# Block-sparse attention feeding a Fourier-mix MLP: the gate product of half the head pairs in 16-bit matmuls instead of float32

## The chip, the cores and the metric

The kernel runs on one NeuronCore of a Trainium2 chip. The metric is the device time of one execution, in microseconds; lower is better. The engines run side by side, each through its own queue in order: TensorE (PE in the profile, its weight loads PEld) multiplies into PSUM; VectorE (DVE), ScalarE (ACT) and GpSimd (POOL) work element by element; SyncE (SP) issues most DMAs.

## What is computed

For 4 batches and 8 heads, with 768 positions and 64 dimensions, attention in which a query sees the causal part of its own block of 64 positions and of up to three other blocks that a gate picks:

```python
k_rep = k.reshape(B, H, n_blocks, block, D).mean(axis=3)          # 12 block means
gate_scores = np.einsum('bhsd,bhnd->bhsn', q, k_rep)              # the gate product
gate_scores = np.where(causal, gate_scores, -1000000000.0)
top_idx = np.argsort(gate_scores, axis=-1)[..., -top_k:]          # top_k = 3
...                                                               # mask from top_idx and own block
attn = softmax(0.125 * q @ k.T, masked);  x = attn @ v            # heads side by side: (4, 768, 512)
X = np.fft.fft(np.fft.fft(x, axis=1), axis=2)
u = x + np.real(X)
un = (u - mean(u)) / sqrt(var(u) + 1e-6)
out = u + np.maximum(un @ w_ch1, 0.0) @ w_ch2                     # 512 -> 2048 -> 512
```

Inputs and output are float32. The choice of blocks is discrete: a gate score that changes its rank changes the output, so the kernel keeps the gate product in float32 while all other products are in 16 bits.

## The kernel before

Two heads of one batch make a pair; 16 pairs (kk = 0 to 15, four to a batch) are worked one after the other, 128 partitions holding 2 x 64 head dimensions. The stages of a pair are spread over three turns of the loop over pairs, so that each engine has work of several pairs at hand:

- stage_A (two turns ahead): TensorE transposes k and q of the pair, three blocks of 128x128 at a time, into PSUM tiles tp. VectorE copies q out as float32, qT (L264), and sums k over blocks of 64, kr12 (L270); two small copies lay these sums out as kr24, one head beside the other with zeros between (L275). ScalarE casts k to 16 bits into kI (L282, for the first seven pairs VectorE takes one of the four, L280). GpSimd casts qT into qg (L267), the 16-bit operand of the scores, one for each head.
- stage_B (two turns ahead, after stage_A): the gate product g, five matmuls of 128 rows of qT (weights) with kr24 (24 columns moving), all float32 (L291; block row 0 needs none). VectorE adds the causal constant (L294), finds the largest eight of each 12 (L301), and makes a 0/1 mask gmp of blocks that are dropped (L303, L306).
- stage_C (one turn ahead): TensorE transposes gmp into gt; VectorE copies it into 12 extra rows of qg (L315). The scores' matmul then adds -60000 to dropped blocks through 12 extra rows of kI that hold -60000 in the columns of one block each.
- stage_S: the scores of a head in three sections of 896 columns, ScalarE's exponential with scale 0.125 into ptl (L349). The causal diagonal is masked by a matmul for pairs up to 6 and on VectorE after (L355).
- stage_AV: ptl times v into av (L370), divided by the row sum on VectorE (L374, L375), into x.

When a batch's four pairs are done, its second half is queued: sums and differences on GpSimd and VectorE (fs, ft, fo, fc; L383 to L389), the Fourier products (za, ya; mx; stage_S1 and stage_S2), u and its statistics on VectorE (L459, L461, L462), the reciprocal root of the variance on GpSimd (stage_N, down to rstd and nmr, L483 to L490), the normalised x on VectorE and ScalarE (L493, L497), its transposes (unt, L506), and the two products of the MLP (ha and hb, L522; ch, L536), with their evictions (L525 on ScalarE, L527 and L539 on VectorE).

The order on TensorE and GpSimd is written out by the program: the loop over pairs emits the stages, and between them a planner, `filler`, hands out units of the second half of earlier batches. It keeps a clock of estimated costs (`feed.now`), by which units that depend on others become ready; `main(stage, cost, ...)` emits a stage and moves that clock by its cost. VectorE, ScalarE and SyncE are ordered by a scheduler.

PSUM has eight banks: four rotate among all tiles with tag ps (tp, g, gt, av, unt, ha, hb, ch, mx, ...), two double ones hold the scores. A tile's buffer comes free when its last reader is done; which earlier tile's buffer a new one gets is fixed when the program is built.

Of the kernel before, what the change touches and what calls it, by code (L numbers as in the profile page):

```python
# [12 lines left out]
F16 = mybir.dt.float16  # L13
# [3 lines left out]
AF = mybir.ActivationFunctionType  # L17
# [101 lines left out]
def kernel(  # L119
# [24 lines left out]
    MULT = mybir.AluOpType.mult  # L144
    ADD = mybir.AluOpType.add
# [6 lines left out]
    psump = ctx.enter_context(tc.tile_pool(name="psum", bufs=4, space=bass.MemoryType.PSUM))  # L152
    apool = ctx.enter_context(tc.tile_pool(name="attn", bufs=2))
    bpool = ctx.enter_context(tc.tile_pool(name="bat", bufs=1))
    spool = ctx.enter_context(tc.tile_pool(name="small", bufs=8))

    def pst(shape, name, dtype=FP, tag="ps", bufs=None):
        return psump.tile(shape, dtype, tag=tag, name=name, bufs=bufs)

    def const(shape, dtype, name):  # L160
        return cpool.tile(shape, dtype, tag=name, name=name)
# [25 lines left out]
    qg_t = [[const([128, S], F16, f"qg_{e}_{sl}") for sl in range(3)] for e in range(2)]  # L187
    warm = const([128, 512], F16, "warm")
    kr24_t = [const([128, 2 * NB], FP, f"kr24_{sl}") for sl in range(2)]
    gmp_t = [const([128, NST - 1, 2, 32], F16, f"gmp_{sl}") for sl in range(2)]  # L190


    EARLY = 7

    feed = Feed()
    P = [dict() for _ in range(NK)]
# [29 lines left out]
    def pool_after(t):  # L226
        nc.gpsimd.tensor_copy(out=dummyp[0:1, 0:1], in_=t[0:1, 0:1])
# [19 lines left out]
    def stage_A(kk, who, g):  # L247
        d = P[kk]
        src = d["qn"] if who == 0 else d["kn"]
        if who == 0 and g == 0:  # L250
            d["qt"] = apool.tile([128, S], FP, tag="qT32", name=f"qT32_{kk}")
            d["qg"] = [qg_t[e][kk % 3] for e in range(2)]
        if who == 1 and g == 0:
            d["kI"] = [kI_t[e][kk % 3] for e in range(2)]
            d["kr12"] = spool.tile([128, NB], FP, tag="kr12", name=f"kr12_{kk}", bufs=2)
            d["kr24"] = kr24_t[kk % 2]
        ps = pst([128, 3, 128], f"tp_{kk}_{who}_{g}")
        for i in range(3):
            nc.tensor.transpose(ps[:, i, :],  # L259
                                src[:, 3 * g + i, :, :].rearrange("p h d -> p (h d)"), id32)  # L260
        flat = ps.rearrange("p a c -> p (a c)")
        cols = slice(384 * g, 384 * (g + 1))
        if who == 0:
            nc.vector.tensor_copy(out=d["qt"][:, cols], in_=flat)  # L264
            if g == 1:
                for e in range(2):
                    nc.gpsimd.tensor_copy(out=d["qg"][e][0:64, :],  # L267
                                          in_=d["qt"][64 * e:64 * e + 64, :])
        else:
            nc.vector.tensor_reduce(out=d["kr12"][:, 6 * g:6 * g + 6],  # L270
                                    in_=ps.rearrange("p a (x c) -> p a x c", x=2),
                                    axis=mybir.AxisListType.X, op=ADD)
            if g == 1:
                for e in range(2):
                    nc.vector.tensor_copy(out=d["kr24"][64 * e:64 * e + 64, NB * e:NB * (e + 1)],  # L275
                                          in_=d["kr12"][64 * e:64 * e + 64, :])
            for e in range(2):
                dst, src_ = d["kI"][e][0:64, cols], flat[64 * e:64 * e + 64]
                if kk < EARLY and g == 1 and e == 1:
                    nc.vector.tensor_copy(out=dst, in_=src_)  # L280
                else:
                    nc.scalar.copy(out=dst, in_=src_)  # L282
# [3 lines left out]

    def stage_B(kk):
        d = P[kk]
        gps = pst([128, NG, 2 * NB], f"g_{kk}")
        for st in range(1, NST):  # L290
            nc.tensor.matmul(gps[:, st - 1, :], d["qt"][:, 128 * st:128 * (st + 1)], d["kr24"],  # L291
                             start=True, stop=True)
        gsb = apool.tile([128, NG, 2, NB], FP, tag="gsb", name=f"gsb_{kk}")
        nc.vector.tensor_tensor(out=gsb.rearrange("p s e n -> p s (e n)"), in0=gps,  # L294
                                in1=cz24[:, 1:NST, :], op=ADD)
        gmp = gmp_t[kk % 2]
        d["gmp"] = gmp
        mx8 = spool.tile([128, NG, 2, 8], FP, tag="mx8", name=f"mx8_{kk}", bufs=2)
        for st in range(NG):
            for e in range(2):  # L300
                nc.vector.max(out=mx8[:, st, e, :], in_=gsb[:, st, e, :])  # L301
        gm = gmp[:, :, :, 0:NB]
        nc.vector.tensor_tensor(out=gm, in0=gsb,  # L303
                                in1=mx8[:, :, :, 2:3].to_broadcast([128, NG, 2, NB]),
                                op=mybir.AluOpType.is_lt)
        nc.vector.tensor_tensor(out=gm, in0=gm, in1=oth24[:, 1:NST, :, :], op=MULT)  # L306

    def stage_C(kk):
        d = P[kk]
# [24 lines left out]
    def stage_S(kk, e, s):  # L334
        d = P[kk]
        if s == 0:
            d.setdefault("pt", {})[e] = apool.tile([128, 3 * SEC], F16, tag=f"ptl{e}",
                                                   name=f"ptl_{kk}_{e}")
        pt = d["pt"][e]
        sp = pst([128, 1024], f"sc_{kk}_{e}_{s}", tag="sc", bufs=2)  # L340
        by_pe = kk < EARLY
        for (jt, a0, a1, co) in SECS[s]:
            diag = by_pe and a0 == 128 * jt
            nc.tensor.matmul(sp[:, co:co + (a1 - a0)],  # L344
                             d["kI"][e][0:76, 128 * jt:128 * (jt + 1)],
                             d["qg"][e][0:76, a0:a1], start=True, stop=not diag)
            if diag:
                nc.tensor.matmul(sp[:, co:co + 128], id16, ltri, start=False, stop=True)  # L348
        nc.scalar.activation(out=pt[:, SEC * s:SEC * (s + 1)], in_=sp[:, 0:SEC], func=AF.Exp,  # L349
                             scale=0.125)  # L350
        if s == 2 and not by_pe:
            um = ut01.rearrange("p (o c) -> p o c", o=1).to_broadcast([128, 3, 128])
            for dg in (pt.rearrange("p (t c) -> p t c", t=3)[:, :, 0:128],
                       pt[:, 384:].rearrange("p (t c) -> p t c", t=3)[:, :, 384:512]):
                nc.vector.tensor_tensor(out=dg, in0=dg, in1=um, op=MULT)  # L355
# [235 lines left out]
    def main(fn, cost, *a):  # L591
        fn(*a)
        feed.spend(cost)
# [6 lines left out]
    with tc.manual_schedule(engines={mybir.EngineType.PE, mybir.EngineType.Pool}):  # L600
# [52 lines left out]
        for kk in range(NK):  # L653
            for p in range(6):
# [70 lines left out]
```

## Time and profile before

| | us |
|---|---|
| runs shown | 345.65, 347.63, 347.56; median 347.56 |
| the profiled execution | 346.12 |
| its span in the profile | 344.3 |
| granted TensorE clock, mean over the span | 0.979 of full |
| product g, 160 records in all | TensorE 20.6 busy, weight loads 20.5 |
| qT copies, 32 in all (VectorE) | 16.6, 547 ns each |
| qg casts, 32 in all (GpSimd) | 27.2, 849 ns each |
| kI casts, 57 on ScalarE | 27.0, 473 ns each |

How to read it: the span is that of one execution taken by the hardware profiler. Each line of a group gives the source line, the engine and operation, what is written and read, the number of instructions, their summed busy time and the mean of one. A float32 matmul appears as two records with a weight load each, so the five matmuls of a pair's g are ten. The chain of waits is followed back from the last instruction: at each step to what released it, or to the instruction before it on the same engine. "Idle before, releaser" names what an engine waited for. The products g of pairs 8 to 15 start on the chain at 89.27, 109.82, 131.23, 152.22, 170.69, 191.40, 212.87 and 233.25 us.

### The profile page before, as it was taken

The page shows a single profiled execution, that of the slowest core. Times are in us where ns is not written, and L with a number is a line of the kernel's source. Part 1 is how long each engine was busy: PE and PEld are TensorE (multiplying, and loading weights), DVE is VectorE, ACT ScalarE, POOL GpSimd, SP SyncE. Part 2 cuts the span into 40 slices and gives each one's busy share as a digit, 9 for nine tenths or more (in the row PEclk, how much of TensorE's full clock was granted, in tenths as well). Part 3 has the DMA queues.
Part 4 walks back from the last instruction along what each step waited for, and adds up shares of the span by engine and source line. Part 5 has one row for each costly group of instructions (what it writes and reads, how often), then busy time and mean ns, then how long its engine had stood idle before and what let it go on. Part 6 is the DMA issues. An engine that isn't in the chain of part 4 may idle for free.

```text
span 344.3 us, 6929 instructions
## 1 busy us (share of the span) xinstructions
PE 320.4 (93%) x2688; PEld 210.2 (61%) x2688; DVE 229.1 (67%) x701; ACT 172.7 (50%) x259; POOL 93.5 (27%) x177
## 2 busy tenths in 40 slices
PE   7899994998899989999999989899999999899995
PEld 3577772886766666566566766556666655456442
DVE  2788889788565779887566688986544868533211
ACT  3177885497874853454375653442566210344000
POOL 8435664244543020342215030161012100200000
PEclk9999998799699999999999999999999999999999
DMA  9999999966498440433523000011000011100021
GB/s 173 197 211 208 261 183 219 147 143 138 80 172 144 82 93 17 107 107 89 143 48 74 20 2 30 32 44 51 32 0 2 5 58 61 62 2 0 32 89 64
DMA packets 85312, 31.18 MB, mean 91 GB/s; under 512 B 77736, under 2 KB 81136, under 8 KB 85280
## 3 DMA queue, kind: packets, MB, share of 16 engines
q1 hardware_dynamic: 79984, 25.88, 33.2%
q0 software_dynamic: 3552, 4.40, 8.1%
q10 hardware_dynamic: 1744, 0.46, 0.7%
q8 instruction: 21, 0.34, 0.4%
q14 instruction: 11, 0.09, 0.1%
HBM read 28.63 MB, written 6.29 MB: 101 GB/s over the span
## 4 chain that ended last, share of the span: by engine, by line
PE 74%; DVE 12%; ACT 4%; POOL 4%; issue 3%; DMA 2%; ACTq 0%; POOLq 0%; DVEq 0%
PE ch L536 21%; PE ha L522 15%; PE hb L522 8%; PE sc L344 8%; PE g L291 5%; PE av L370 5%; PE tp L259 3%; ACT kI L282 2%; DVE kr L270 2%; DVE mx L301 2%; DMA qn<-in_q_dram 2%; PE gt L312 1%; PE ya L424 1%; PE mx L448 1%; DVE bst L461 1%
## 5 line engine op out<-in xcount | busy, mean ns | idle before, releaser
L349 ACT ACTIVATE ptl<-sc 128x896 f16<-128x896 f32 x96 | 87.1, 917 | 51.9 <-PE sc L344 42.1
L536 PE MATMUL ch<-w_sb,hT 128*128 128x512 f16 x384 | 91.2, 379 | 1.3 <-DVE u L539 1.2
L522 PEld LDWEIGHTS <-w_sb 128*128 128x128 f16 x512 | 48.8, 98 | 35.7 <-issue 0.7
L522 PE MATMUL ha<-unT,w_sb 128*128 128x512 f16 x256 | 65.7, 379 | 0.1
L344 PE MATMUL sc<-qg,kI 76*128 76x512 f16 (+3 forms) x256 | 55.7, 309 | 4.1 <-ACT ptl L349 4.0
L536 PEld LDWEIGHTS <-hT 128*128 128x128 f16 x384 | 36.1, 97 | 36.8 <-issue 1.4
L525 ACT ACTIVATE hT<-ha 128x512 f16<-128x512 f32 x64 | 38.1, 597 | 30.7 <-PE ha L522 30.7
L527 DVE TENSOR_SCALAR hT<-hb 128x256 f16<-128x256 f32 x64 | 26.9, 422 | 36.1 <-PE hb L522 36.1
L522 PE MATMUL hb<-unT,w_sb 128*128 128x256 f16 x256 | 38.4, 273 | 0.3 <-ACT unT L509 0.3
L383 POOL TENSOR_TENSOR fs<-x 128x384 f16<-128x384 f16 x12 | 11.2, 929 | 100.2 <-DVE x L375 100.2
L344 PEld LDWEIGHTS <-kI 76*128 76x128 f16 x256 | 24.5, 101 | 19.4 <-issue 2.9
L282 ACT CAST kI<-tp 64x384 f16<-64x384 f32 x57 | 27.0, 473 | 11.7 <-DVE kr L270 10.7
L267 POOL CAST qg<-qT 64x768 f16<-64x768 f32 x32 | 27.2, 849 | 19.7 <-DVE qT L264 18.7
L539 DVE TENSOR_TENSOR u<-ch,u 128x512 f32<-128x512 f32 x24 | 16.5, 688 | 21.6 <-PE ch L536 21.3
L370 PE MATMUL av<-v,ptl 128*128 128x65 f16 x672 | 26.2, 195 | 0.0
L370 PEld LDWEIGHTS <-ptl 128*128 128x128 f16 x672 | 24.8, 98 | 2.1 <-issue 0.2
L497 ACT ACTIVATE x<-u,nmr,rstd 128x512 f16<-128x512 f32 x12 | 8.9, 803 | 26.8 <-POOL nmr L490 26.8
L270 DVE TENSOR_REDUCE kr<-tp 128x6 f32<-128x384 f32 x32 | 17.0, 546 | 7.0 <-PE tp L259 6.9
L291 PEld LDWEIGHTS g<-kr,qT 128*128 128x128 f32 x160 | 20.5, 200 | 1.3 <-issue 0.3
L291 PE MATMUL g<-kr,qT 128*128 128x24 f32 x160 | 20.6, 271 | 0.0
L348 PE MATMUL sc<-ltri,id 128*128 128x128 f16 x84 | 18.6, 222 | 0.0
L375 DVE TENSOR_TENSOR x<-av,rcp 128x384 f16<-128x384 f32 x32 | 17.8, 557 | 1.0
(91 smaller groups left out, 406.5 us busy)
## 6 DMA issues: line engine op xcount, KB each, us to landing
vn<-in_v_dram SPq DMA_DIRECT2D x32, 192.0 KB, 3.6
out_dram<-u SPq DMA_DIRECT2D x24, 256.0 KB, 2.0
kn<-in_k_dram SPq DMA_DIRECT2D x30, 192.0 KB, 4.0
qn<-in_q_dram SPq DMA_DIRECT2D x30, 192.0 KB, 4.1
w_sb<-in_moe_w_ch_dram POOLq DMA_DIRECT2D x8, 256.0 KB, 6.9
w_sb<-in_moe_w_ch_dram POOLq DMA_DIRECT2D x4, 512.0 KB, 8.5
cs_sb<-c_CS SPq DMA_DIRECT2D x1, 289.5 KB, 4.8
ss_sb<-c_SS SPq DMA_DIRECT2D x1, 289.5 KB, 3.6
```

Source lines behind the costliest of these rows:

```text
L267: nc.gpsimd.tensor_copy(out=d["qg"][e][0:64, :], in_=d["qt"][64 * e:64 * e + 64, :])
L270: nc.vector.tensor_reduce(out=d["kr12"][:, 6 * g:6 * g + 6], in_=ps.rearrange("p a (x c) -> p a x c", x=2), axis=mybir.AxisListType.X, op=ADD)
L282: nc.scalar.copy(out=dst, in_=src_)
L291: nc.tensor.matmul(gps[:, st - 1, :], d["qt"][:, 128 * st:128 * (st + 1)], d["kr24"], start=True, stop=True)
L344: nc.tensor.matmul(sp[:, co:co + (a1 - a0)], d["kI"][e][0:76, 128 * jt:128 * (jt + 1)], d["qg"][e][0:76, a0:a1], start=True, stop=not diag)
L348: nc.tensor.matmul(sp[:, co:co + 128], id16, ltri, start=False, stop=True)
L349: nc.scalar.activation(out=pt[:, SEC * s:SEC * (s + 1)], in_=sp[:, 0:SEC], func=AF.Exp, scale=0.125)
L370: nc.tensor.matmul(av[:, st, 0:65], pt[:, o:o + 128], d["v16"][:, e, jt, 0:65], start=(cnt == 0), stop=(cnt == 20))
L522: nc.tensor.matmul(hp_, w1_sb[:, dt, 128 * it:128 * (it + 1)], unT[:, dt, c0:c1], start=(dt == 0), stop=(dt == NDT - 1))
L525: nc.scalar.activation(out=hT[:, c0:c1], in_=hp_, func=AF.Relu)
L527: nc.vector.tensor_scalar(out=hT[:, c0:c1], in0=hp_, scalar1=0.0, scalar2=None, op0=mybir.AluOpType.max)
L536: nc.tensor.matmul(cps, x["hT"][it][:, 128 * st:128 * (st + 1)], w2_sb[:, it, :], start=(it == 0), stop=(it == NIT - 1))
```

## The change

For pairs 8 to 15 (SPLIT = 8) the gate product is done in 16-bit matmuls. q is multiplied by 64 and split into a high part, rounded to f16, and a low part, the f16 of the rest; the block sums of k likewise. The high and low parts of q share the bytes of the float32 tile qT. The parts of k stand side by side, 24 columns each, in a new tile krx, and each block row takes two matmuls, one for either part of q, over all 48 columns, summed in PSUM; VectorE adds the two halves of 24 columns. All four cross terms are so kept. ScalarE makes the high part of q from PSUM, VectorE the low part. qg is cast from the high part, and so is 64 times larger: the mask gets the factor 64 too, and the exponential's scale is divided by it. The planner's cost of stage_B is 0.35 instead of 1.05 for these pairs; a pool of small tiles has 6 buffers instead of 8; GpSimd's wait before the first w2 loads is on the low part.

```diff
-    spool = ctx.enter_context(tc.tile_pool(name="small", bufs=8))
+    spool = ctx.enter_context(tc.tile_pool(name="small", bufs=6))
...
+    krx_t = [const([128, 2, 2 * NB], F16, f"krx_{sl}") for sl in range(2)]
...
+    SPLIT = 8
+    QS = 64.0
+    STT = nc.vector.scalar_tensor_tensor
...
+            if kk >= SPLIT:
+                parts = d["qt"].bitcast(F16)
+                d["qh"], d["ql"] = parts[:, 0:S], parts[:, S:2 * S]
...
-            nc.vector.tensor_copy(out=d["qt"][:, cols], in_=flat)
+            if kk < SPLIT:
+                nc.vector.tensor_copy(out=d["qt"][:, cols], in_=flat)
+            else:
+                nc.scalar.activation(out=d["qh"][:, cols], in_=flat, func=AF.Copy, scale=QS)
+                STT(out=d["ql"][:, cols], in0=flat, scalar=QS, in1=d["qh"][:, cols], op0=MULT, op1=SUB)
             if g == 1:
                 for e in range(2):
                     nc.gpsimd.tensor_copy(out=d["qg"][e][0:64, :],
-                                          in_=d["qt"][64 * e:64 * e + 64, :])
+                                          in_=d["qt" if kk < SPLIT else "qh"][64 * e:64 * e + 64, :])
...
-            if g == 1:
+            if g == 1 and kk < SPLIT:
                 for e in range(2):
                     nc.vector.tensor_copy(out=d["kr24"][64 * e:64 * e + 64, NB * e:NB * (e + 1)],
                                           in_=d["kr12"][64 * e:64 * e + 64, :])
+            elif g == 1:
+                d["krx"] = krx_t[kk % 2]
+                for e in range(2):
+                    r, c = slice(64 * e, 64 * e + 64), slice(NB * e, NB * (e + 1))
+                    hi, lo = d["krx"][r, 0, c], d["krx"][r, 1, c]
+                    nc.vector.tensor_scalar(out=hi, in0=d["kr12"][r, :], scalar1=QS, scalar2=None, op0=MULT)
+                    STT(out=lo, in0=d["kr12"][r, :], scalar=QS, in1=hi, op0=MULT, op1=SUB)
...
+            gps = pst([128, NG, 2, 2 * NB], f"g_{kk}")
+            krx = d["krx"].rearrange("p o n -> p (o n)")
+            for st in range(1, NST):
+                for n, part in enumerate((d["qh"], d["ql"])):
+                    nc.tensor.matmul(gps[:, st - 1, :, :].rearrange("p o n -> p (o n)"),
+                                     part[:, 128 * st:128 * (st + 1)], krx, start=(n == 0), stop=(n == 1))
+            nc.vector.tensor_tensor(out=gsf, in0=gps[:, :, 0, :], in1=cz24[:, 1:NST, :], op=ADD)
+            nc.vector.tensor_tensor(out=gsf, in0=gps[:, :, 1, :], in1=gsf, op=ADD)
...
-        nc.vector.tensor_tensor(out=gm, in0=gm, in1=oth24[:, 1:NST, :, :], op=MULT)
+        if kk < SPLIT:
+            nc.vector.tensor_tensor(out=gm, in0=gm, in1=oth24[:, 1:NST, :, :], op=MULT)
+        else:
+            STT(out=gm, in0=gm, scalar=QS, in1=oth24[:, 1:NST, :, :], op0=MULT, op1=MULT)
...
-                             scale=0.125)
+                             scale=0.125 if kk < SPLIT else 0.125 / QS)
...
+        for t in krx_t:
+            nc.gpsimd.memset(t, 0.0)
...
-                    main(stage_B, 1.05, kk + 2)
+                    main(stage_B, 1.05 if kk + 2 < SPLIT else 0.35, kk + 2)
...
-                pool_after(P[kk + 2]["qt"])
+                pool_after(P[kk + 2]["qt" if kk + 2 < SPLIT else "ql"])
```

In the built program TensorE's stream is the same as before but for g: where a pair from 8 on had five float32 matmuls it has ten 16-bit ones. ScalarE has two more instructions for each of these pairs and VectorE three, GpSimd two more in all.

More of the change, by code (lines that the diff above doesn't have):

```diff
@@ L288, in stage_B @@
         d = P[kk]
[L289 to L292, printed above, removed]
         gsb = apool.tile([128, NG, 2, NB], FP, tag="gsb", name=f"gsb_{kk}")
-        nc.vector.tensor_tensor(out=gsb.rearrange("p s e n -> p s (e n)"), in0=gps,
-                                in1=cz24[:, 1:NST, :], op=ADD)
+        gsf = gsb.rearrange("p s e n -> p s (e n)")
+        if kk < SPLIT:
+            gps = pst([128, NG, 2 * NB], f"g_{kk}")
+            for st in range(1, NST):
+                nc.tensor.matmul(gps[:, st - 1, :], d["qt"][:, 128 * st:128 * (st + 1)], d["kr24"],
+                                 start=True, stop=True)
+            nc.vector.tensor_tensor(out=gsf, in0=gps, in1=cz24[:, 1:NST, :], op=ADD)
+        else:
+            gps = pst([128, NG, 2, 2 * NB], f"g_{kk}")
+            krx = d["krx"].rearrange("p o n -> p (o n)")
+            for st in range(1, NST):
+                for n, part in enumerate((d["qh"], d["ql"])):
[3 more added lines that the diff above has]
+            nc.vector.tensor_tensor(out=gsf, in0=gps[:, :, 1, :], in1=gsf, op=ADD)
         gmp = gmp_t[kk % 2]
@@ L305, in stage_B @@
                                 op=mybir.AluOpType.is_lt)
-        nc.vector.tensor_tensor(out=gm, in0=gm, in1=oth24[:, 1:NST, :, :], op=MULT)
+        if kk < SPLIT:
+            nc.vector.tensor_tensor(out=gm, in0=gm, in1=oth24[:, 1:NST, :, :], op=MULT)
+        else:
+            STT(out=gm, in0=gm, scalar=QS, in1=oth24[:, 1:NST, :, :], op0=MULT, op1=MULT)
     def stage_C(kk):
```

## The prediction

> **What bounds the kernel.** I read the page's busy shares first, then its chain of work that ended last, then that chain in order of time around each gate product (line L291, tile g), and last the waits and the timeline where the chain leaves TensorE.
>
> ```profile
> PE 320.4 (93%) x2688; PEld 210.2 (61%) x2688; DVE 229.1 (67%) x701; ACT 172.7 (50%) x259; POOL 93.5 (27%) x177
> ...
> PEclk9999998799699999999999999999999999999999
> ...
> PE 74%; DVE 12%; ACT 4%; POOL 4%; issue 3%; DMA 2%; ACTq 0%; POOLq 0%; DVEq 0%
> ...
> L370 PEld LDWEIGHTS <-ptl 128*128 128x128 f16 x672 | 24.8, 98 | 2.1 <-issue 0.2
> ...
> L291 PEld LDWEIGHTS g<-kr,qT 128*128 128x128 f32 x160 | 20.5, 200 | 1.3 <-issue 0.3
> ```
>
> TensorE is busy 93% of the span and carries 74% of the chain; the clock row dips twice. A float32 weight load takes 200 ns, a 16-bit one of the same size 98 ns. The 160 records of g are ten for each of 16 pairs. The chain in order of time shows the two settings in which a g can lie:
>
> ```profile
> 87.72 0.58 PE sc L344
> ...
> 89.27 2.07 PE g L291 x10
> ...
> 170.25 0.44 PE hb L522 x4
> 170.69 1.03 PE g L291 x10
> 171.72 0.87 PE ha L522 x4
> ...
> 178.34 0.64 PE av L370 x21
> ...
> 212.87 1.03 PE g L291 x10
> ...
> 214.37 0.69 DVE u L459
> 215.07 0.73 DVE mx L301 x10
> ...
> 218.95 0.61 DVE u L539
> 219.56 0.04 issue
> 219.61 1.02 PE ch L536 x4
> ```
>
> At 170.69 (pair 12) g has matmuls directly before and after it: there, shorter is earlier. At 212.87 (pair 14) the chain leaves TensorE 1.5 us later and VectorE sets the pace until 219.61. At 89.27 (pair 8) the half clock doubles g.
>
> **The change part by part.** *Gate product.* Removed per pair: 1.03 us. Added: ten 16-bit matmuls with 128-column weights, 48 columns moving. The nearest row is av, the same pairing with 65 columns: 21 in 0.64 us, 30 ns each, so 0.30 us for ten. The far bound is gt (five transposes in 0.39 us on the chain, 78 ns each): 0.78 us. I take av's, nearest in shape: a gain of 0.73 us where TensorE is continuous (0.25 by the far bound).
>
> The Trainium skill ("TensorE: Matmul & The Clock Gate", section "Back-to-back issue gap") speaks against this: it gives some 81 ns for each sustained load and matmul pair at 128 columns. By that the ten would cost 0.81 us and the pair gain 0.22; av's 30 ns here contradicts it for narrow operands, so the row decides.
>
> *q.* Two VectorE copies (547 ns each) become two ScalarE activations 128x384 and two VectorE operations reading PSUM and the new 16-bit part. VectorE: 128x384 with two sources is x<-av,rcp, 557 ns: no difference. ScalarE: between kI's cast (64x384, 473 ns) and hT (128x512, 597 ns), say 0.5 us each, 1.0 per pair; ScalarE is idle half the span, so what counts is where they stand in its queue (below). GpSimd's qg now waits for ScalarE's half; its 16-bit read may cost less or more than the 849 ns of now, and in the timeline qg of pair 9 is cast by 103.7 while its scores start two pairs later. GpSimd's casts of v and, at pairs 8 and 9, the w2 loads (issued at 89.4 and 104.7) stand behind it and slip by the same 1 us; w2's product starts at 132.5.
>
> *k and the mask.* Per pair VectorE gets two more 64x12 operations (186 ns as kr's copies), a second add of 128x120 (283 ns as the first) and a fused multiply (217 to 283 ns, was 217): 0.7 us, all in order before whatever stands behind.
>
> *The rest.* The exponential's scale is a constant, no cost. Two small GpSimd memsets before the kI loads cost about 0.15 us each by the v memsets (128 to 152 ns); those loads are issued by 5.5 us and first used at 17.8. Six instead of eight small buffers touch rcp and bst, which the same engine consumes within a microsecond. The estimate of g in the planner's clock changes no place in TensorE's stream: in the built program it is as before but for g itself.
>
> Now pair by pair, as the built order has the new operations.
>
> - Pairs 9, 11, 12, 13 (g at 109.82, 152.22, 170.69, 191.40): TensorE continuous. Transposes end 1.5 to 3 us before the next user of their buffer, in which ScalarE's and VectorE's halves (1.6 us) fit: at pair 13 transposes end at 182.4 and the user starts at 184.23, while VectorE today frees that buffer at 184.05. If the cover is gone it costs some 0.3 us a pair. 4 x 0.73 = 2.9 gained.
> - Pair 8: ScalarE's two stand behind the three x of L497 (which wait for GpSimd's nmr and end at 86.87) and ahead of the exponential that releases the scores at 87.72. So scores start 1.0 later, g at 90.2, and at half clock it lasts 0.6 instead of 2.07: it ends at 90.8 instead of 91.33. Gain 0.4 (bounds: 1.5, loss 1.0).
> - Pair 14: VectorE is saturated from 209.3 to 223.7, so the shorter g ends in a wait. Its own addition ahead of u L539 is 0.3; and the built program puts the ch that waits there at 219.61 in a buffer freed by ScalarE's kI casts, which start at 219.2 today and would start 0.4 later; two take 0.95. ch at 220.6: loss 1.0 (bounds 0 and 1.3).
> - Pair 10 likewise: mx, released today by u L459 at 137.97, waits for two kI casts that start at 137.6: 138.6, loss 0.6 (bounds 0, 0.9).
> - Pair 15: the second q operation moves behind VectorE's x (ends 228.95), and VectorE arrives about 1.2 late at the unT copies after it; of 0.73 I keep 0.5 (bounds 0.73, 0).
>
> Sum: -0.4 - 2.9 + 0.6 + 1.0 - 0.5 = -2.2 us. Nothing after 240 contains the change; the last 100 us only start earlier.
>
> The profiled execution took 346.1 us (span 344.3 plus 1.8); the three runs have a median of 347.6, 345.65 to 347.63. I set the sum against the middle of the two, 346.8: **344.6 us**. By the bounds this case runs from -3.8 (nothing lost at 10 and 14) to +0.6 (gt's price for the matmuls): 343.0 to 347.4.
>
> **Rivals.**
>
> *All eight pay.* If the losses at 10, 14 and 15 don't arise, because VectorE catches up in earlier time that TensorE frees, and 8 gains as the others: 8 x 0.73 = 5.8, so 341.0. For it: 93% busy. Against: 1.25 us of idle already before ch at 219.61 behind VectorE.
>
> *One more half-clock interval.* The rows of the granted clock show 0.50 from 57.0 to 63.8 and from 87.7 to 94.6, both after stretches where TensorE was less than 60% busy (1.9 us of the last 3.4, and 1.5). Pair 14's idle of 1.25 us grows to about 2.1. One such interval of 6.8 us at half clock loses 3.4: -2.2 + 3.4 = +1.2, 348.0. Against it: 12.5 to 16 us is no busier (2.3 of 4 us between 12 and 16) and keeps its clock.
>
> The same page of the Trainium skill ("The two states you'll see") asks for a whole idle window of about 3.4 us before the clock halves; by it 2.1 us of idle costs nothing and the sum stays as it is. The rows here show it halved with some work in the window, so I keep the rival.
>
> *Slower.* The mechanism is the same queueing, decided at two places: ScalarE's casts hold buffers at 138 and at 220 so long that TensorE falls below that share in both, and two intervals follow: -2.2 + 6.8 = +4.6, 351.4. It decides once the waits there exceed some 2 us each; today they are 0.38 and 1.25, which speaks against it.
>
> That the change doesn't do what it says can be ruled out: the built program has ten 16-bit matmuls for each of these pairs and no float32 product.
>
> **How the numbers follow.** Forecast 0.52, all eight pay 0.21, one interval 0.15, slower 0.12. One per cent, about what a measurement of this kernel tells from none, is 3.5 us. Faster by more: all of the second and 0.14 of the forecast, whose lower bound is -3.8: 0.35. Slower: 0.12. Within: 0.53. The range leaves out the slower case and some 0.07 at the lower end of the second: 340.8 to 348.2. The likeliest case alone has 343.0 to 347.4.
>
> **What would show it.** g of pairs 8 to 15 at about 0.30 us on the chain, 0.6 at half clock; 30 ns a matmul. TensorE's busy time down some 5.5 us, VectorE's up by 5 to 6, ScalarE's by about 8. The time between g of pair 9 and g of pair 10 shorter by 0.7; between g of 14 and g of 15 not shorter. Wrong if g's ten take over 0.6 at full clock, if ch near 218 waits no longer than today, or if the clock row has a third dip.

## The result, and the profile after

The changed kernel takes 345.19 us (median of 22 runs, 343.56 to 348.69), the kernel before in the same comparison 346.62 us (22 runs, 345.65 to 350.14). The ratio is 0.9952, with a 95% interval from 0.9935 to 0.997: some 1.5 us less, which is real and lies within the 1% that was called no change. Forecast were 344.6 us, with 340.8 to 348.2. The profiled execution took 346.51 us with a span of 344.7; nine of the 22 had a mean granted clock of 0.98 (median 344.2 us), the other thirteen 0.968 to 0.975 (345.59), and the profiled one is of the thirteen.

The page's busy shares, clock row and chain by engine:

```profile
PE 316.1 (92%) x2688; PEld 204.9 (59%) x2688; DVE 234.0 (68%) x725; ACT 178.9 (52%) x275; POOL 94.0 (27%) x179
...
PEclk9989998799899989999999999999999999999999
...
PE 69%; DVE 24%; ACT 3%; issue 2%; POOL 2%; DVEq 0%; ACTq 0%
```

TensorE's busy time went down by 4.3 us, VectorE's up by 4.9, ScalarE's by 6.2 (against before's 320.4, 229.1 and 172.7). On the chain TensorE's share fell from 74 to 69% while VectorE's doubled from 12 to 24%. The clock row has four dips where before had two. One, in the 3rd slice (17.7 to 21.1 us), lies ahead of everything that the change touches on TensorE, and the float32 kernel of a later experiment (e5_u_early) has it too; the other, in the 15th (123.2 to 126.6 us), is told of below. The new product, from the groups by line:

```profile
L322 PE MATMUL g<-krx,qT 128*128 128x48 f16 x80 | 3.5, 188 | 0.0
```

On the chain in order of time it takes 0.25 us for ten where the clock is full, and 0.40 for pair 8. The chain around pair 8:

```profile
85.48 2.06 DVE x L526 x3
...
87.55 0.48 DVE qg L348
...
88.68 1.00 PE av L403 x21
...
91.53 0.40 PE g L322 x10
```

av needs a buffer that qg's copies free, and these stand behind three x: av starts at 88.68 where before it ran at 84.81, and so g starts 2.3 us later than before's 89.27 (1.55 of it had arisen before g of pair 7, where the changed kernel's profile has its early dip), but lasts 0.40 instead of 2.07.

Around pair 10 the chain in order of time shows what nothing in the prediction had named:

```profile
121.16 1.79 DVE ptl L388 x2
...
123.34 1.13 PE ya L457 x6
```

VectorE's two diagonal-mask products took 1.79 us on the chain; in before two of this size at the same place took 0.62. Beside them, in the timeline of GpSimd (start, duration, line, operation; in brackets the idle time before and what ended it):

```profile
120.95 1.79 POOL L280 COPY qg<-qT 64x768 f16<-64x768 f16 x2 [2.54 <-ACT qT L276]
```

and in that of before:

```profile
123.39 1.70 POOL L267 CAST qg<-qT 64x768 f16<-64x768 f32 x2 [4.61 <-DVE qT L264]
```

The copies start 2.4 us earlier, because ScalarE's half of q releases them and not VectorE's, which stands behind the masks in VectorE's queue. So they run beside the masks and no longer after them. In the timeline the first mask runs from 121.08 to 122.05 and the second from 121.98 to 122.95; the copies beside them end at 121.84 and 122.74. Each mask ends 0.21 us after the copy beside it. In the table by windows (length, then busy time of TensorE, weight loads, VectorE, ScalarE, GpSimd, then the granted clock) TensorE starves, and the clock follows:

```profile
120.00:122.00 2.00, 0.73 (x9) 0.57 (x7) 2.00 (x5) 0.87 (x2) 0.99 (x2) 1.00 0.31 73
122.00:124.00 2.00, 0.66 (x5) 0.61 (x5) 2.00 (x5) 0.00 (x0) 1.57 (x2) 0.81 0.55 124
124.00:126.00 2.00, 2.00 (x13) 1.56 (x12) 1.18 (x3) 1.50 (x3) 0.00 (x0) 0.50 0.64 145
```

In before the same three windows have TensorE busy for 1.09, 1.55 and 2.00 us at a clock of 1.00.

To see what each pair gained, I take the time from the first matmul of one pair's g to that of the next from TensorE's timeline. From pair 9 on these distances repeat within 0.07 us from profile to profile where nothing changes and the clock holds (from 7 to 9, where the clock is halved, within 0.4), while the start of g of pair 7 wanders by itself: 76.31 in before, 77.86 after, and 74.88 to 80.05 in the experiments that leave it alone. So only what follows it is compared. "TensorE alone" is an experiment told of below; "end" is the end of the span.

| from g of pair | before, us | after | TensorE alone |
|---|---|---|---|
| 7 to 9 | 33.35 | 32.22 | 31.77 |
| 9 to 10 | 21.41 | 23.47 | 20.51 |
| 10 to 11 | 21.02 | 21.02 | 20.55 |
| 11 to 12 | 18.43 | 18.43 | 18.11 |
| 12 to 13 | 20.72 | 19.94 | 19.80 |
| 13 to 14 | 21.47 | 20.68 | 20.56 |
| 14 to 15 | 20.37 | 20.64 | 20.12 |
| 15 to end | 111.22 | 110.44 | 110.38 |
| sum | 267.99 | 266.84 | 261.80 |

So the profiled execution gained 1.15 us behind g of pair 7: 1.13 at pair 8, 0.78 or 0.79 each at 9 (hidden in the 23.47), 12, 13 and 15, nothing at 10 and 11, minus 0.27 at 14, and minus 2.84 between pairs 9 and 10, where by an estimate the stretched masks account for some 1.2 (1.79 less 0.62) and the lower clock for the rest (half of the 3.4 us at 0.50).

The 1.13 at pair 8 is less firm than the others. The half-clock stretch there lasted 6.8 us in before (87.8 to 94.6) and 3.4 in this profile (89.1 to 92.5). A later run whose pairs 8 and 9 are the same as here (e4_five_pairs) had the long stretch again and took 32.62 from 7 to 9; four others (e1_qg_late, e2_no_k_low, e6_five_pairs_u_early, e7_all_late_u_early) had the short one and 32.23 to 32.26. So some 0.4 of the 1.13 goes with the shorter stretch, which the change doesn't bring each time.

### The profile page after: what moved, and what is told of

The parts are those of the page before. It is cut to its first block, busy times and chain, and to the rows that moved or that the text cites. A ratio compares the mean times of both kernels' runs of the same rounds, so it can differ in the third digit from the quotient of the medians.

```text
span 344.7 us, 6968 instructions
## 1 busy us (share of the span) xinstructions
PE 316.1 (92%) x2688; PEld 204.9 (59%) x2688; DVE 234.0 (68%) x725; ACT 178.9 (52%) x275; POOL 94.0 (27%) x179
## 4 chain that ended last, share of the span: by engine, by line
PE 69%; DVE 24%; ACT 3%; issue 2%; POOL 2%; DVEq 0%; ACTq 0%
PE ch L569 17%; PE ha L555 15%; PE hb L555 8%; PE sc L377 8%; PE av L403 5%; PE tp L268 3%; PE g L314 3%; PE warm L356 3%; DVE bst L494 2%; DVE kr L283 2%; ACT kI L302 2%; DVE mx L331 2%; DVE u L492 2%; DVE x L526 2%; PE ya L457 2%
## 5 line engine op out<-in xcount | busy, mean ns | idle before, releaser
L572 DVE TENSOR_TENSOR u<-ch,u 128x512 f32<-128x512 f32 x24 | 16.5, 686 | 21.1 <-PE ch L569 20.8
L388 DVE TENSOR_TENSOR ptl<-ptl,ut 128x384 f16<-128x384 f16 x36 | 13.6, 412 | 8.4 <-ACT ptl L382 8.4
L494 DVE BATCH_NORM_STATS2 bst<-u 128x6 f32<-128x512 f32 x24 | 16.6, 690 | 1.1 <-ACT u L490 0.7
L280 POOL COPY qg<-qT 64x768 f16<-64x768 f16 x16 | 14.2, 886 | 10.0 <-ACT qT L276 9.5
```

Source lines behind the costliest of these rows:

```text
L494: nc.vector.bn_stats(out=bst, in_=u_b[:, kt, :])
```

## Experiments

Each was compared with the kernel before in runs on the same chip; the ratio is to that. Theory A, to begin with: TensorE's saving is kept where TensorE is continuous, lost where VectorE sets the pace and is given more to do, and GpSimd's earlier copies cost 1.3 us at pair 10 and the clock dip. The rivals: the clock takes the gain back wherever it arises, or ScalarE's new activations hold the buffers.

**GpSimd's copies back to their old place** (e1_qg_late). A tiny copy that reads the last of VectorE's low half is put in front of them:

```diff
             if g == 1:
+                if kk >= SPLIT:
+                    nc.gpsimd.tensor_copy(out=dummyp[0:1, 0:1], in_=d["ql"][0:1, S - 1:S])
                 for e in range(2):
```

> The 16-bit version with one thing moved: GpSimd's copies of q's high half (qg, 64x768, two a pair) start only when VectorE has written the second low half, as the order of before had it; eight tiny copies are added on GpSimd. Theory A (GpSimd's 16-bit copies that start early run beside VectorE's diagonal-mask products and stretch them: 1.87 us for two near 121 us in the profile of the changed kernel, 0.62 in before; this costs 1.26 us at pair 10 and lets the clock drop there): the two masks near 121 take 0.62 us again, no row of the granted clock is under 0.9 between 118 and 130 us, and the time falls from 345.2 to 343.7 (343.2 to 344.4). Rival B (what stretches the masks is their own data or VectorE's queue; or VectorE's lag is hidden there): the masks keep over 1.5 us or the time stays at 345.2 +-0.4. Rival C (the later qg holds up the scores of the next pair): the time is over 345.6.

Measured: 343.61 us, ratio 0.9903 (0.9882 to 0.9924). The masks, in VectorE's timeline, and the windows of the same stretch:

```profile
123.28 0.62 DVE L390 TENSOR_TENSOR ptl<-ptl,ut 128x384 f16<-128x384 f16 x2
```

```profile
122.00:124.00 2.00, 0.93 (x10) 0.77 (x9) 2.00 (x6) 0.87 (x2) 0.00 (x0) 1.00 0.18 42
124.00:126.00 2.00, 1.72 (x19) 1.58 (x19) 2.00 (x5) 1.02 (x3) 0.71 (x2) 1.00 0.68 154
```

The masks take 0.62 again, GpSimd is idle beside them, the clock stays at 1.00, and from g of pair 9 to that of pair 10 there are 20.62 us instead of 23.47. The time is that of theory A; by the medians the edit gains 1.6 us, by the two profiles behind g of pair 7 it is 2.69 (264.15 against 266.84). This edit, which moves no work between engines, is worth as much again as the whole change.

**Without the low part of k** (e2_no_k_low): the operations that make the low part and the second add are left out.

```diff
-                    STT(out=lo, in0=d["kr12"][r, :], scalar=QS, in1=hi, op0=MULT, op1=SUB)
...
-            nc.vector.tensor_tensor(out=gsf, in0=gps[:, :, 1, :], in1=gsf, op=ADD)
```

> The 16-bit version without the low part of k's block sums: the two 64x12 operations that make it and the second add of 128x120 are left out for pairs 8 to 15 (the cross terms with k's low part are missing from the gate); TensorE's matmuls, ScalarE's work and q's low part are as in the changed kernel. VectorE loses 2 x 0.165 + 0.276 = 0.6 us a pair. Theory A (at pairs 10, 11 and 14 VectorE sets the pace, and what it gets in addition is paid there, while elsewhere it is hidden): g of pair 10 to g of pair 11, 11 to 12 and 14 to 15 are each 0.4 to 0.6 us shorter than in the changed kernel, the other distances the same; 343.6 (343.2 to 344.2). Rival B (ScalarE's two activations a pair, which are still here, are what holds the buffers): 345.2 +-0.4, distances as in the changed kernel. Rival C (TensorE is the bound everywhere, and the saving is lost in the clock): 345.2 with the third dip still there.

Measured: 344.53 us, ratio 0.9928 (0.9904 to 0.9953). From pair 10 to 11 20.59 and from 14 to 15 20.19, 0.43 and 0.45 less than the changed kernel; but 11 to 12 stayed at 18.42. That is a good half of what theory A expected: at pair 11 VectorE's additions are not the reason. The masks and the dip at pair 10 are still there (23.44 from 9 to 10), and the interval of the time overlaps the changed kernel's, so the distances carry the reading. They hold more than VectorE's work, though. In the changed kernel, between pairs 10 and 11, a product mx waits, and ScalarE casts kI beside it:

```profile
140.50 0.27 PE L481 MATMUL mx<-cd_sb,yR 128*128 128x256 f16 x1 [0.98 <-DVE krx L295]
```

```profile
139.51 1.93 ACT L302 CAST kI<-tp 64x384 f16<-64x384 f32 x4
```

In this run:

```profile
137.09 0.27 PE L479 MATMUL mx<-cd_sb,yR 128*128 128x256 f16 x1 [0.53 <-DVE u L490]
```

In the changed kernel mx starts when two of the four casts are done (some 140.45); krx, which the profile names, ends at nearly the same time (140.47) but reads no PSUM tile. In this run the casts begin at 136.54, and mx starts before two of them are done, right after VectorE's u, so it has another buffer. Against g of pair 10 it starts 0.44 earlier; VectorE's u ends only 0.19 earlier, and the other 0.25 is the wait for ScalarE's casts. The ch of pair 14 shows the same two parts (0.19 and 0.26). So the rival that ScalarE holds the buffers is right for a part, by its old casts and not by its new activations.

**VectorE's additions alone** (e3_vec_cost), on the float32 product, and the same **with two adds held in place** (e3b_vec_cost_pinned):

```diff
+                    if kk >= 8:
+                        nc.vector.tensor_copy(out=xk[64 * e:64 * e + 64, e, :],
+                                              in_=d["kr12"][64 * e:64 * e + 64, :])
...
+        if kk >= 8:
+            nc.vector.tensor_tensor(out=xg, in0=gps, in1=cz24[:, 1:NST, :], op=ADD)
```

> The kernel before (float32 product, q copied by VectorE), with only VectorE's additions of the change put in at pairs 8 to 15: two more 64x12 operations after kr and a second add of 128x120 reading g; their results are not used. Nothing is saved on TensorE. Theory A (the additions are paid at the pairs where VectorE sets the pace, 10, 11 and 14, and hidden elsewhere): 0.4 to 0.6 us longer at each of these three, 346.6 + 1.5 = 348.1 (347.6 to 348.6). Rival B (hidden at all pairs, so that the changed kernel's lost savings come from ScalarE's activations or GpSimd's copies): 346.6 +-0.4. Rival C (paid at all eight): 346.6 + 8 x 0.6 = 351.4.

Measured: 345.58 us, ratio 0.9968 (0.9941 to 0.9994): faster with more work, which no theory had. Pair 10 to 11 took 20.31 (before 21.02) and 14 to 15 19.93 (20.37). VectorE's order isn't written out in this kernel but made by a scheduler, and the additions changed it. Its timeline in this run:

```profile
144.79 0.69 DVE L546 TENSOR_TENSOR u<-ch,u 128x512 f32<-128x512 f32 x1
147.16 1.97 DVE L500 TENSOR_SCALAR x<-u,stat,rstd 128x512 f16<-128x512 f32 x3 [1.67 <-POOL rstd L495]
```

and in before:

```profile
147.54 1.96 DVE L493 TENSOR_SCALAR x<-u,stat,rstd 128x512 f16<-128x512 f32 x3 [2.35 <-POOL rstd L488]
149.43 0.68 DVE L539 TENSOR_TENSOR u<-ch,u 128x512 f32<-128x512 f32 x1
```

An add u, ready, stood behind three x that wait 2.35 us for GpSimd's rstd; with the additions it stands ahead and fills the wait. Theory K: this swap made the gain. It was tried by itself on the kernel before (e5_u_early), the three x being issued after the add:

```diff
-            nc.vector.tensor_tensor(out=x["u"][:, st, :], in0=cps, in1=x["u"][:, st, :], op=ADD)
+            u = nc.vector.tensor_tensor(out=x["u"][:, st, :], in0=cps, in1=x["u"][:, st, :], op=ADD)
+            if late:
+                with tc.issue_after(u.ins):
+                    norm_x(late.pop())
```

> The kernel before (float32 product at all pairs) with one swap in VectorE's order, at two places (after pair 10's and after pair 14's product): one add u, whose matmuls are done, stands ahead of the three x that wait for GpSimd's rstd instead of behind them. No work is added or removed. Theory K (the run with VectorE's additions was faster than before only because the scheduler made this same swap, which fills an idle of 2.35 us of VectorE): g of pair 10 to g of pair 11 is 0.6 to 0.7 us shorter than before's 21.02, the time from g of pair 14 to g of pair 15 or from there to the end 0.3 to 0.5 shorter, and the time falls by 1.1 (0.7 to 1.4) from its before. Rival (the swap is worth nothing, and the gain of that run came from other shifts of its order or from the spread of runs): distances as in before within 0.1, same time +-0.4.

Measured: ratio 0.9987 (0.9969 to 1.0006). Pair 10 to 11 took 20.75, 0.27 less; 14 to 15 stayed at 20.37. The swap is worth a third of what theory K had, and the interval of the time includes no gain at all. And the additions with the swap excluded, the two adds being held behind the x of the next batch:

```diff
+            if (b, st) in ((0, 1), (1, 2)):
+                with tc.issue_after(X[b + 1]["last"].ins):
+                    add_u()
```

> The kernel before with VectorE's additions of the change (two more 64x12 operations and a second 128x120 add per pair from 8 on, results not used), and with the two adds u held behind the x of their batch as in before, so that the swap is out. Theory A (the additions are paid where VectorE sets the pace): g10 to g11 longer than before's 21.02 by 0.3 to 0.6, g14 to g15 longer than 20.37 by 0.2 to 0.6, the rest unchanged: slower than its before by 0.5 to 1.2. Rival B (hidden everywhere): distances as before within 0.1, same time +-0.4.

Measured: ratio 1.0007 (0.9983 to 1.0031); 10 to 11 20.94, 11 to 12 18.47, 14 to 15 20.54, that is -0.08, +0.04 and +0.17. So 0.6 us more work a pair on VectorE costs next to nothing on the long product, in the order that the scheduler then finds; on the short one leaving it out gave 0.43 and 0.45 back, of which 0.19 each is VectorE's u that ends earlier and the rest the buffer. The 0.71 and 0.44 of the first run are neither the swap's nor the additions', but of the order as a whole, in which the adds u of mx and the bst moved too; which move does it isn't settled.

**TensorE's side alone** (e8_gain_alone). This asks the question the other way round: the product reads the upper 16 bits of the float32 tiles where they lie, so no other engine gets anything; the lower bits are left out.

```diff
+        qb, kb = d["qt"], d["kr24"]
+        if kk >= 8:
+            qb, kb = (t.bitcast(mybir.dt.bfloat16).rearrange("p (n o) -> p n o", o=2)[:, :, 1] for t in (qb, kb))
         for st in range(1, NST):
-            nc.tensor.matmul(gps[:, st - 1, :], d["qt"][:, 128 * st:128 * (st + 1)], d["kr24"],
+            nc.tensor.matmul(gps[:, st - 1, :], qb[:, 128 * st:128 * (st + 1)], kb,
```

> The kernel before with TensorE's side of the change alone: for pairs 8 to 15 the gate product reads only the upper 16 bits of q and of k's block sums where they lie (as bfloat16, every second 16-bit word): five 16-bit matmuls a pair in place of five float32 ones in two passes each. The lower bits are left out of the gate. No other engine gets or loses an instruction. TensorE saves about 0.9 us a pair (1.03 less five of some 25 to 30 ns). Theory A (at pairs 10, 11 and 14 TensorE's time isn't what counts, whatever VectorE is given): 0.9 shorter for the product of pairs 9, 12, 13 and 15, 1.5 to 2 around pair 8; g10 to g11 and g14 to g15 at most 0.2 shorter than before's 21.02 and 20.37, g11 to g12 within 0.1 of 18.43; 346.4 - 5.3 = 341.1 (340.5 to 342.2). Rival B (these three pairs lose their gain only to the change's additions on VectorE and ScalarE): all eight pay, 0.9 shorter there too, 338.4 (337.8 to 339.3).

Measured: 340.92 us, ratio 0.9827 (0.9788 to 0.9866), where theory A had 341.1. The last column of the table has its distances: 0.84 to 0.92 gained at pairs 9, 12, 13 and 15, 1.58 around 8, but only 0.47, 0.32 and 0.25 at 10, 11 and 14 (theory A had at most 0.2, 0.1 and 0.2), though nothing else changed. The chain in order of time between pairs 10 and 11 of this run shows who sets the pace there:

```profile
130.29 0.60 DVE u L462
...
135.42 0.27 PE mx L451
...
144.78 0.21 POOL rstd L491
...
145.02 1.96 DVE x L496 x3
146.98 0.60 DVE u L542
```

From 128 to 135.4 and from 141.2 to 149.4 the chain runs on VectorE and GpSimd: a batch's statistics and normalisation. A shorter g only makes TensorE wait longer for it.

**Only the pairs that pay** (e4_five_pairs): `SPLIT` becomes a set.

```diff
-    SPLIT = 8
+    SPLIT = (8, 9, 12, 13, 15)
...
-            if kk >= SPLIT:
+            if kk in SPLIT:
```

> The 16-bit product only for pairs 8, 9, 12, 13 and 15; pairs 10, 11 and 14 as in before. Theory A (the profile of the changed kernel keeps 1.1 us at pair 8, 0.78 each at 9, 12 and 13, 0.4 at 15, nothing at 10, 11 and 14, and loses 1.3 at pair 10's masks and 0.3 at 14): the sum of what is kept, 3.8 us, comes out whole: 346.6 - 3.8 = 342.8 (342.3 to 343.6), faster than all eight pairs. Rival B (the three left pairs gain as well, only the profiled execution hid it by its third clock dip): slower than all eight pairs by up to 3 x 0.78, 345.2 to 347.5. Rival C (whatever is gained is given back at the next place where VectorE sets the pace, so the number of pairs hardly matters): 345.2 +-0.4.

Measured: 342.16 us, ratio 0.9873 (0.9853 to 0.9894), better than theory A's 342.8. Pair 9 to 10 takes 20.63 (GpSimd's copies of pair 10 wait for VectorE again), 10 to 11 21.02 and 11 to 12 18.44 as in before. Against all eight pairs with the late copies (0.9903) the intervals overlap, and behind g of pair 7 the two profiles take 264.23 and 264.15 us: most of what the five pairs gain over the changed kernel is the end of the collision at pair 10. With the swap of u and x (the edit shown above), for the five pairs and for all eight with the late copies:

> The 16-bit product at pairs 8, 9, 12, 13 and 15 (the earlier run of this gave a ratio of 0.9873) and the swap of u and x at the two places. Theory K: the two gains add, 0.9873 - 1.1/347 = 0.984 (0.983 to 0.9855), 341.1. Rival (VectorE's slack that the swap makes is the same that the five pairs already use): 0.987 +-0.001.

> The 16-bit product at all eight pairs with GpSimd's qg late (the earlier run of this gave 0.9903) and the swap of u and x at the two places. Theory (VectorE sets the pace at 10, 11 and 14 whatever TensorE saves there, so what the swap frees on VectorE is gained, and no more): 0.9903 - 1.1/347 = 0.987 (0.986 to 0.989), slower than the five pairs with the swap by 1.0 to 1.5 us; g11 to g12 still 18.4. Rival (with VectorE relieved the three pairs 10, 11 and 14 pay their 0.78 each as well): 0.982 or less, faster than the five pairs with the swap.

Measured: 341.32 us, ratio 0.9851 (0.9822 to 0.9879), and 342.03 us, ratio 0.9879 (0.984 to 0.9917). Both are near the theory's numbers; the intervals of the two overlap, so that the five pairs beat the eight here isn't shown by the times, but the distances 10 to 11 (20.75 and 20.65) and 11 to 12 (18.36 and 18.34) show that these two pairs still don't pay their 0.78. From 14 to 15 it is 20.38 and 22.29: in the profile of all eight pairs the clock fell there (0.65 over 218 to 220 us, 0.50 over 220 to 222), after four microseconds in which TensorE was busy for 1.88. That is the profiled execution alone; how often the clock falls there in the others isn't shown.

**Two more pairs** (e9_seven_pairs_u_early):

```diff
-    SPLIT = (8, 9, 12, 13, 15)
+    SPLIT = (6, 7, 8, 9, 12, 13, 15)
```

> The 16-bit product at pairs 6, 7, 8, 9, 12, 13 and 15 with the swap of u and x (without pairs 6 and 7 it gave a ratio of 0.9851). In before TensorE is busy 11.98 of the 12 us from 64 to 76, in which g of pair 6 lies; after g of pair 7 the chain leaves TensorE for VectorE and GpSimd. Theory (a pair pays where TensorE is continuous behind its product and doesn't where VectorE sets the pace): pair 6 pays 0.78, pair 7 nothing or up to 0.5 loss; ratio 0.983 to 0.9845. Rival (VectorE, which is busy 9.4 of those 12 us, is late for it): 0.985 or more.

Measured: 346.36 us, ratio 0.9979 (0.9956 to 1.0003): the whole gain gone, though g of pair 6 to that of pair 7 took 9.88 instead of 10.59. The planner places the other work on TensorE by its own clock, and with 0.35 instead of 1.05 for these two pairs it placed it elsewhere. By windows, this run and then the one with five pairs:

```profile
86.00:96.00 10.00, 9.30 (x79) 7.17 (x79) 6.13 (x28) 9.93 (x18) 6.83 (x10) 0.66 0.55 93
96.00:98.67 2.67, 0.07 (x1) 0.00 (x0) 2.67 (x6) 1.13 (x3) 2.61 (x4) 1.00 1.22 193
```

```profile
86.00:96.00 10.00, 8.54 (x99) 6.33 (x100) 6.65 (x28) 9.93 (x19) 5.67 (x9) 0.83 0.56 93
96.00:98.67 2.67, 2.67 (x19) 1.69 (x18) 1.84 (x6) 2.21 (x4) 1.48 (x3) 1.00 1.21 194
```

TensorE has nothing to do for 2.6 us where with five pairs it is full, and the clock falls behind it (0.57 over 100 to 104 us, 1.00 with five pairs). From 8 to 9 it is 22.44 instead of 18.76; 9 to 10 (21.86) and 11 to 12 (19.84) are longer as well. With the old cost for pairs 6 and 7, which leaves TensorE's order as it was, once for the seven pairs and once without pair 7:

```diff
-                    main(stage_B, 1.05 if kk + 2 not in SPLIT else 0.35, kk + 2)
+                    main(stage_B, 1.05 if kk + 2 not in (8, 9, 12, 13, 15) else 0.35, kk + 2)
```

> The same as the run with seven pairs (6, 7, 8, 9, 12, 13, 15, and the swap of u and x), but with the planner's cost of the products of pairs 6 and 7 left at 1.05, so that TensorE's order is that of the five pairs. Theory (the seven pairs lost their gain, 0.9979 against 0.9851, because the smaller planned cost moved the w1 and unT blocks on TensorE: the profile had 22.44 us from g8 to g9 where the five pairs have 18.76; the products themselves paid, 9.88 from g6 to g7 against 10.60): 0.9851 - 0.7/346.5 = 0.983 (0.9815 to 0.9845), g8 to g9 again under 19.3. Rival (pair 7's work on VectorE and ScalarE in front of the chain of the first batch costs it): g8 to g9 over 20, ratio over 0.99.

> The same without pair 7 (6, 8, 9, 12, 13, 15). Theory: pair 6 pays 0.7 as in the run with seven pairs, g6 to g7 9.9 us, everything behind it as with five pairs: 0.983 (0.9815 to 0.9845), equal to the run with pair 7 or better by up to 0.5 us. Rival (what pair 6 saves is taken back at the chain of VectorE and GpSimd behind g of pair 7): 0.985.

Measured: 340.26 us, ratio 0.9817 (0.9791 to 0.9844), with pair 7, and 340.60 us, ratio 0.9828 (0.9802 to 0.9854), without; pair 8 to 9 is back at 19.19 and 18.75. The rival of the first falls: it was the placement. The rival of the second, that what pair 6 saves is taken back, doesn't: its 0.985 lies in the interval, and 6 to 7 is now 10.49 and 10.48, only 0.1 less than before. The spans of the three profiles are 339.2, 339.0 and 339.1 (five pairs). So a gain of the two more pairs over the five isn't shown; their intervals overlap. All three are faster than both kernels, and the version with seven pairs has the lowest median of all, 1.8% under the kernel before.

## Why the prediction was right, and where it was not

The total came out well, 344.6 against 345.19, but by luck: of the profile's distances, 2.85 us were lost at a place that the prediction didn't name and 0.73 of pair 11 didn't come, while the losses at 10 and 14 had been put 1.33 too high and the gains at 8, 12, 13 and 15 (with 9's product) 1.2 too low.

- **Price of the product.** Forecast 30 ns a matmul, 0.30 us for ten; measured 0.25, a gain of 0.78 where 0.73 stood. av's row was the right one to take. The section of the Trainium skill that was weighed against it ("TensorE: Matmul & The Clock Gate", "Back-to-back issue gap") also has a table by columns with an issue floor of some 25 ns up to 64 columns; this agrees with the 25 ns here. Its 81 ns for sustained pairs is given for 128 moving columns, so it says nothing of 48; unt here, with 128 columns of weights and 128 moving, takes 55 (four in 0.22 us on the chain of before).
- **Pairs 9, 12, 13: continuous TensorE, the saving kept.** Right: 0.78, 0.78, 0.79 (pair 9's from the run with late copies, 20.62 against 21.41).
- **Pair 11, counted with them: wrong.** It gained nothing. I had read from the chain, which lay on TensorE from 151 to 171, that nothing else was late. TensorE's timeline in before and after shows how near it was:

```profile
152.09 1.27 PE L291 MATMUL g<-kr,qT 128*128 128x24 f32 x10
...
157.05 0.38 PE L506 MATMUL unt<-id,x 128*128 128x128 f16 x4
```

```profile
154.57 0.41 PE L322 MATMUL g<-krx,qT 128*128 128x48 f16 x10
...
159.52 0.38 PE L539 MATMUL unt<-id,x 128*128 128x128 f16 x4 [0.43 <-ACT kI L302]
```

From g to this unt it is 4.96 us before and 4.95 after; it stands behind ScalarE's kI casts, and these behind VectorE's kr. In before VectorE's timeline shows no idle time from 147.54 to 157.06, and TensorE was at this unt 0.42 us after the start of the sc ahead of it, where the same three sc take 0.38 elsewhere (153.42 to 153.80): it had some 0.04 us to spare. A chain names who came last, not by how little: the slack of the next engine should have been read from VectorE's timeline, as was done for pair 14. The run with TensorE's side alone puts a number on it: 0.32 of 0.92 to be had.
- **Pair 10, loss 0.6: the mechanism right, the size not.** mx waits for two kI casts as was said (the lines are with the run without the low part of k), 0.98 instead of 0.38 us. But the shorter g had brought TensorE there earlier: against g, mx starts only 0.05 later than before, and the distance to pair 11 is 21.02 before and after. The saving was lost, and nothing on top.
- **Pair 14, loss 1.0: too large.** Measured 0.27. The ch waits where it was said to, and the casts are what frees its buffer, as the timelines of TensorE and ScalarE after and then ScalarE's before show:

```profile
220.78 1.02 PE L569 MATMUL ch<-w_sb,hT 128*128 128x512 f16 x4 [1.85 <-DVE krx L295]
```

```profile
218.97 0.92 ACT L382 ACTIVATE ptl<-sc 128x896 f16<-128x896 f32 x1 [3.10 <-PE sc L377]
219.78 1.93 ACT L302 CAST kI<-tp 64x384 f16<-64x384 f32 x4
```

```profile
218.40 0.92 ACT L349 ACTIVATE ptl<-sc 128x896 f16<-128x896 f32 x1 [2.66 <-PE sc L344]
219.21 1.93 ACT L282 CAST kI<-tp 64x384 f16<-64x384 f32 x4
```

The first two of the four casts end at some 220.75, when ch starts (220.78). (VectorE's krx, which the profile names, ends then too, as at pair 10.) But I had held the casts 0.4 later than in before. Against g, which starts 0.91 later in this execution, they start 0.34 earlier: the exponential ahead of them waits for scores, and these came earlier because g was shorter. The saving was spent on the way to the wait and not added to it.
- **Pair 8, gain 0.4 of bounds 1.5 and -1.0.** Measured 1.13, or some 0.7 with a half-clock stretch as long as before's. The half clock made g's saving 1.67; about 0.5 was lost, and the chain lays it to av's buffer behind x and qg on VectorE, a wait that wasn't named. ScalarE's place in the queue, which was named, is not on the chain there.
- **Pair 15, 0.5.** Measured 0.78; the lateness of VectorE after it was hidden.
- **GpSimd's qg: "waits for ScalarE's half", with later starts as the only cost.** This is the step that failed most. It starts earlier, not later, and so beside VectorE's masks. Measured with the late copies: 2.85 us from pair 9 to 10, of which by the estimate above some 1.2 are the masks and the rest clock.
- **Rivals.** All eight pay: false even for TensorE's side alone. One more half-clock interval: it came, in the profiled execution, but at pair 10 rather than 14, and half as long; priced at 3.4, it cost about 1.6. At pair 14 it came in the profile of all eight pairs with late copies and the swap. A third dip was named as what would show the forecast wrong, and the one at pair 10 did show the missing cost; the one at 17.7 us has nothing to do with it. VectorE's additions, rated at 0.3 us at pair 14 and as part of 10's loss: alone they cost at most 0.17.
- **Busy times.** Forecast were 5.5 us less on TensorE, 5 to 6 more on VectorE and 8 more on ScalarE; measured 4.3, 4.9 and 6.2, all in the direction that was said and smaller.

So of some 6.2 us that TensorE's side is worth, the distance from pair 9 to 10 took 2.96 (23.47 against 20.51; 2.85 of it the masks and the clock), pairs 10, 11 and 14 another 1.31, pair 8 0.45, and the ten matmuls in place of five at 12, 13 and 15 0.32. That leaves the 1.15 of the profiled execution.

## What to carry to other kernels

When an operation moves to another engine, look at what it releases earlier, not only at what it delays: an off-path engine that starts sooner can run beside a neighbour that it used to follow. A chain on one engine doesn't show the slack of the next; where that engine's timeline has no idle time, a saving is worth only the slack. Here, leaving out the pairs that can't use the change cost nothing, but it isn't shown to be faster than keeping them once the collision is gone. And where a planner or scheduler places work by estimated costs, hold the order fixed while measuring, or the order is what is measured.

## What the hardware showed beyond that

- Two VectorE products of two 16-bit sources in SBUF, 128x384, take 0.62 us alone and 1.79 while GpSimd copies 64x768 of f16 (GpSimd itself takes 1.79 for its two instead of 1.70). The Trainium skill ("GPSIMD Engine Reference", "1. Specifications") says that GpSimd shares its SBUF interfaces with VectorE and that VectorE instructions with two SBUF inputs contend; the runs agree, and put the price near three times for VectorE; each product ended 0.21 us after the copy beside it, as if it waited for the copy. The same shows beside other work of GpSimd: a mask at 144.61, while GpSimd's fs runs until 145.29, takes 0.90 us and again ends 0.21 after it, its twin at 146.03 takes 0.34.
- GpSimd's copy of f16 to f16 is no faster than its cast from float32: median 824 against 822 ns for 64x768.
- The clock falls with some work in the window too, and the share of work alone doesn't tell when. It was halved from 123.2 us in the changed kernel, after 3.4 us (119.8 to 123.2) in which TensorE was busy for 0.93; busy for 2.64 of four (before, 120 to 124) it kept its clock. Between these, at pair 14, TensorE was busy for 1.55 of 3.4 us in two runs with nearly the same work: the changed kernel kept its clock (218.8 to 222.2), all eight pairs with late copies and the swap lost it (215.2 to 218.6).
